# An attention and mixture-of-experts kernel: first expert's preparation in finer steps, its weights split off GpSimd, last pair's rows and the routing's fill in another order

## The chip, the cores and the metric

One core of one Trainium2 chip runs the whole kernel in one launch. The metric is the device time in microseconds (us) of that core; the kernel before takes 794.57 us, the median of three runs (792.56 to 796.7). The engines are named as the profile names them: PE is TensorE (PEld its weight loads), DVE is VectorE, ACT is ScalarE, POOL is GpSimd, SP is SyncE, which here only starts transfers.

## The reference

Three layers are computed one after the other on four sequences (b) of 576 tokens with 512 channels.

```python
# 1. attention, 8 heads of 64: only keys within tau of the row's best score are kept
scores = q @ k.T / 8;  keep = scores >= max(scores) - tau
x = softmax(where(keep, scores, -1e9)) @ v
# 2. mixture of experts: 8 experts, one expert per token
logits = x @ w_gate;   local = sigmoid(x @ w_local)
for s in range(S):                       # a scan along the sequence
    e = argmax(logits[s]) if s == 0 or local[s] < 0.5 else e
    out[s] = softmax(logits[s])[e] * (relu(x[s] @ w1[e]) @ w2[e])
# 3. a second mixture, of 4 causal attention heads, 2 picked per token
```

The choice of the expert is a scan: a token either takes its own best expert or the expert of the token before it.

## The kernel before

**Stage 1, attention (`stage1`).** 32 heads are worked as 16 pairs p. All work of a pair is written as small functions, and each is put at a time on a step axis by `at(g, f, ...)`; the pair p starts at step g = 9p, and the table `W` (line 385) gives the offsets. All functions are then called in the order of their steps, so every engine's queue has that order, and no engine overtakes in its own queue. For a pair, `scores` (PE) gives 9 score tiles, `rowmax` and `keep` (DVE) and `expo` (ACT) make the kept probabilities, `tp` (PE) and `tp_ev` (ACT) transpose them, `av` (PE) multiplies by the values, `rows` (PE, line 334) turns the result into token rows and the routing's logits beside them, `rows_ev` copies these out, and `norm` (line 358) divides by the softmax sums, stores the rows to `x_dram` in HBM and adds the logits into `L`. Pairs 4b to 4b+3 belong to sequence b, so sequences 0 to 2 are complete when pair 11 is through.

**The early routing (`Route.early`, line 509).** While pairs 12 to 15 run, the routing of sequences 0 to 2 is done in 17 pieces which are hooked into stage 1 at the steps of `EARLY` (line 1566): choose the expert per token (`choose`, line 475), transpose, two scans on DVE (`scan`, `ranks`), `count` and `most` (which expert is worked first), `value` and `place` (a token's place among its expert's), `column`, five `hot` (masks, on POOL) and `invert` (15 small PE matmuls that give the list of tokens of the first tile). From `most` comes the first expert's number, with which `weights0` starts its four 1 MB weight transfers (`W0`); `rows0` gathers the first tile's 256 rows (`R0`), `tx0` transposes them (`TX0`), and `split0` (`S0`) splits four 1024-column pieces of the weights into a high and a low part: ACT rounds (line 803), then POOL subtracts (line 804).

**The routing's end (`Route.main`, line 640).** After the last pair, the fourth sequence is routed: a chain of some 60 small DVE instructions with small PE matmuls between them. To keep PE at work, `fill(i)` puts pieces of the first expert's tile (tile 0) into PE's queue at nine places, `FILL[i]` pieces each. The tile has 32 pieces (`start`, line 1025): 16 of the first matrix (six matmuls of 256 columns) and 16 of the second (three of 512). What is not used up in the chain is done after it, with the transposes of tile 1's rows (`tx`) put between at the counts of `LEFT`. `hT_ev` (line 924) takes a finished block of hidden values out of PSUM and splits it; for blocks 0 and 1 (`HPOOL`) POOL does the subtraction. `SPL` tells at which pieces the other four weight pieces (`w2`, line 970 uses them) are split.

**Then** tiles 1 to 8 (`g1`, `g2`) and stage 3 follow; nothing of them is changed.

The order of the last pair before is: its first 256 rows are made at step 149.66 (`rows` p15, after both halves of `av`), its logits in `norm`, as DVE work, and its rows scaled by POOL in one instruction (line 366).

Of the kernel before, what the change touches and what calls it, by code (L numbers as in the profile page):

```python
# [111 lines left out]
def stage1(tc, nc, K, qT, qx, kT, vp, tau, wgl, x_dram, L, X, hooks=(), npair=NP):  # L112
# [14 lines left out]
    iw = C.tile([128, 4, 146], F32, name="iw")  # L127
    nc.gpsimd.memset(iw[:, :, 128:146], 0.0)
    NQ, NK = 3, 2
    QS = [C.tile([128, 2, S], F32R, name=f"QS{i}") for i in range(NQ)]  # L130

    KK = [C.tile([128, 1216], F32R, name=f"KK{i}") for i in range(NK)]
    KL = [C.tile([128, 1216], F32R, name=f"KL{i}") for i in range(NK)]
    KC = (slice(0, 576), slice(576, 1216))
    QM = [C.tile([128, 2, 128], F32R, name=f"QM{i}") for i in range(NK)]

    PD = [C.tile([128, 128], F32, name=f"PD{i}") for i in range(2)]
    J = C.tile([128, 64], F32, name="J")
# [183 lines left out]
    RC, XR, RW, RT = {}, {}, {}, {}  # L322
# [21 lines left out]
    def rows_ev(p, g):  # L344
        t, n = RT.pop((p, g)), 2 + g
        if g == 0:
            XR[p] = (X.tile([128, 5, 2, 64], F32, name="xr", bufs=2),
                     X.tile([128, 5, 2, 9], F32, name="lg", bufs=2))
        tt = t[:, 0:146 * n].rearrange("p (j x)->p j x", x=146)
        js = slice(2 * g, 2 * g + n)  # L350
        if g == 0:
            RW[p] = P1.tile([128, 5, 146], F32, name="xraw", bufs=1)
        nc.scalar.activation(RW[p][:, js], tt, AF.Copy)
        if p == npair - 1:
            nc.vector.tensor_mul(XR[p][1][:, js], tt[:, :, 128:146].rearrange("p j (a d)->p j a d", a=2),
                                 RC[p][:, js].unsqueeze(3).to_broadcast([128, n, 2, 9]))

    def norm(p):
        b, c = divmod(p, 4)
        r, lg = XR[p]  # L360
        q, last = RW.pop(p), p == npair - 1
        if last:
            logits(p, lg, nc.vector)
# [5 lines left out]
        rv = r.rearrange("p j a d->p j (a d)")  # L369
        nc.sync.dma_start(x_dram[b, 0:512, 128 * c:128 * c + 128].rearrange("(j p) d -> p j d", p=128), rv[:, 0:4])  # L370
        nc.sync.dma_start(x_dram[b, 512:576, 128 * c:128 * c + 128], rv[0:64, 4])
        if not last:
            scaled(lg, q[:, :, 128:146], 9)
            logits(p, lg, nc.gpsimd)
# [22 lines left out]
    for p in range(npair):  # L397
# [18 lines left out]
        at(g + W["diag"], diag, p)  # L416
        for h in range(2):
            at(g + W["tpm"][h], tpm, p, h)
            at(g + W["pmev"][h], tpm_ev, p, h)
            for k in range(5):  # L420
                at(g + W["av"][h], av, p, h, k)
            at(g + W["xt"][h], av_ev, p, h)
            at(g + W["row"][h], rows, p, h)
            at(g + W["rev"][h], rows_ev, p, h)
        at(g + W["keep"][8] + 0.1, sums, p)
        at(g + W["recip"], recip, p)
        at(g + W["rev"][1] + 0.1, norm, p)
# [25 lines left out]
class Route:  # L453
# [21 lines left out]
    def choose(self, bs, e=None):  # L475
# [11 lines left out]
        v.scalar_tensor_tensor(fr[:, :, bs], self.L[:, :, bs, 8], Z_THR, s0[:, :, bs], op0=ALU.is_lt, op1=ALU.max)  # L487
        e.tensor_scalar(U[:, 1, :, bs], bc(fr), -1.0, 1.0, op0=ALU.mult, op1=ALU.add)
        v.tensor_reduce(mx[:, :, bs], l8, axis=AX.X, op=ALU.max)
        v.tensor_tensor(q, l8, bc(mx), op=ALU.is_equal)  # L490
        e.tensor_tensor(q, q, w8, op=ALU.mult)
        v.tensor_reduce(m2[:, :, bs], q, axis=AX.X, op=ALU.max)
        v.tensor_tensor(q, q, bc(m2), op=ALU.is_equal)
        e.tensor_tensor(U[:, 0, :, bs], q, bc(fr), op=ALU.mult)
# [14 lines left out]
    def early(self):  # L509
# [9 lines left out]
        def chosen(*_):  # L519
            gp.tensor_copy(self.io, K["iota128"])  # L520
            gp.tensor_copy(K.identb, K["ident"])
            self.choose(slice(0, 3), gp)
# [20 lines left out]
        def scan(*_):  # L543
            O = T["O"] = self.scratch("O")
            v.tensor_tensor_scan(O[rs], T["A"][rs], T["G"][rs], 0.0, op0=ALU.mult, op1=ALU.add)

        def ranks(*_):
            O = T["O"]
            R = T["R"] = self.scratch("R")
            v.tensor_tensor_scan(R[rs], K["ones"][rs, 0:1].to_broadcast([N, S]), O[rs], 0.0, op0=ALU.mult, op1=ALU.add)  # L550

            T["n8"] = E.tile([32, 8], F32, name="n8")
            v.tensor_scalar(T["n8"][rs], K["selE"][rs], R[rs, S - 1:S], None, op0=ALU.mult)
# [69 lines left out]
        def hot(k):  # L623
            def f(*_):
                for b in range(3):
                    gp.tensor_scalar(self.ln[:, k, b], self.io, self.place[:, k, b:b + 1], K["tok"][:, 4 * k + b:4 * k + b + 1],
# [3 lines left out]
        def invert(xt, _):  # L630
            pi = xt()
            for k in range(15):
# [4 lines left out]
        return [chosen, rows("A", 1), rows("G", 0), rest, scan, ranks, count, most, value, place, column,  # L637
                *[hot(k) for k in range(5)], invert]

    def main(self, fill, first):  # L640
# [9 lines left out]
        nc.gpsimd.memset(O[:, S:640], 0.0)  # L650
        fill(0)
        self.choose(slice(3, 4))
# [14 lines left out]
        A = W.tile([32, S], F32, name="A", tag="AR")  # L667
        nc.scalar.activation(A[:, 0:512], pa[0:32], AF.Copy)
        nc.scalar.activation(A[:, 512:S], px[0:32, 128:192], AF.Copy)
        fill(1)  # L670
        v.tensor_copy(selb, K["selb"][0:32])
# [3 lines left out]
        v.tensor_tensor_scan(R, K["ones"][:32, 0:1].to_broadcast([32, S]), O[:, :S], 0.0, op0=ALU.mult, op1=ALU.add)  # L675
        n = R[:, S - 1:S]
# [3 lines left out]
        fill(2)  # L680
# [13 lines left out]
        fill(3)  # L694
# [8 lines left out]
        fill(4)  # L703
# [30 lines left out]
        fill(5)  # L734
# [5 lines left out]
        first()  # L740
        slot = C.tile([128, 20], I32, name="slot")
# [11 lines left out]
        fill(6)  # L753
# [22 lines left out]
        fill(7)  # L776
# [22 lines left out]
def split_chunk(nc, W, src, t, c):  # L799
    tag = "w1" if c < 4 else "w2"  # L800
# [3 lines left out]
    (nc.gpsimd if (t, c) in POOL else nc.vector).tensor_sub(l, src, h.bitcast(F32))  # L804
    return h, l
# [59 lines left out]
def moe(tc, nc, K, R, E, M, yg, W, ctx):  # L865
# [53 lines left out]
    def split(t, c):  # L919
        wc[t, c] = split_chunk(nc, E if c < 4 else W, R.piece(t, c), t, c)  # L920
# [3 lines left out]
    def hT_ev(t, p, i, n, gp=False):  # L924
# [7 lines left out]
        if gp:  # L932
            r = W.tile([128, 512], F32, name="h", bufs=1).rearrange("p (f t) -> p f t", f=2)
            nc.scalar.activation(r, p, AF.Relu)
            nc.gpsimd.tensor_sub(hl, r, hh.bitcast(F32))
        else:
            nc.vector.scalar_tensor_tensor(hl, p, 0.0, hh.bitcast(F32), op0=ALU.max, op1=ALU.subtract)  # L937
# [87 lines left out]
    def start():  # L1025
        hT[0] = []
        for i in range(4):
            p = P1.tile([128, 512], F32, name="acc", bufs=2)
            for k in range(4):
                for f in range(2):  # L1030
                    h_mm(0, p[:, 256 * f:256 * f + 256], 2 * i + f, k, k == 0 and f == 0)
                if k == 3:
                    hT_ev(0, p, i, 0, i in HPOOL)
                for c in range(4, 8):
                    if SPL[c - 4] == 4 * i + k:
                        lab(split, 0, c)
                yield
        ys[0] = [bank("py") for _ in range(2)]
        for i in range(4):
            for u in range(2):  # L1040
                for f in range(2):
                    y_mm(0, i, u, f)
                    if i == 3 and f == 1:
                        y_ev(0, u)
                    yield

    yield
    pieces = start()
# [11 lines left out]
    for i in range(3):  # L1060
        while left > LEFT[i]:
            next(pieces)
            left -= 1
        lab(tx, 1, i)
        gather()
    for _ in pieces:
        pass
# [95 lines left out]
def stage3(tc, nc, K, ws, xr, fetch, xscale, row, out, nb=B):  # L1163
# [380 lines left out]
    for y in range(2 * nb):  # L1544
# [10 lines left out]
        for h, n in enumerate((5, 10)):  # L1555
# [17 lines left out]
SPL = (0, 5, 13, 14)  # L1573
HPOOL = (0, 1)
# [170 lines left out]
```

## Time and profile before

| | us |
|---|---|
| three runs, median (lowest to highest) | 794.57 (792.56 to 796.7) |
| the profiled execution, its own time | 799.57 |
| its span in the trace | 797.8 |
| PE busy | 748.1 (94% of the span) |
| DVE, ACT, POOL busy | 550.2, 490.2, 282.2 |

The profiled execution is 0.6% above the median of the runs; all times of single instructions come from it. A time in the trace counts from the span's start. Stage 1 fills the span up to about 312 us, the routing's end and the rest of tile 0 the stretch to 360.7 us, tiles 1 to 8 and stage 3 what follows. An idle engine costs nothing unless the engine that sets the end waits for it; TensorE's granted clock (1.00 is 2.4 GHz, 0.50 is 1.2 GHz) stands beside the busy times.

### The profile page before, as it was taken

How to read it: one execution, taken by the hardware profiler on the slowest of the kernel's cores; microseconds unless marked ns; L12 is line 12 of the kernel's file. 1: busy time of each engine (PE TensorE's matmuls, PEld its weight loads, DVE VectorE, ACT ScalarE, POOL GpSimd, SP SyncE). 2: the span in 40 equal slices, each digit the busy share in tenths (PEclk: the TensorE clock that was granted, in tenths of full speed). 3: DMA queues.
4: the chain of work that ended last, by engine and by line, in shares of the span. 5: the costliest groups of instructions: out<-in, count | busy, mean ns of one | idle time of the engine just before them, and what ended most of it. 6: DMA issues, size and time to landing. Idle time of an engine off the chain costs nothing. (4 is left out here: it accounts for less than half of the span.)

```text
span 797.8 us, 14293 instructions
## 1 busy us (share of the span) xinstructions
PE 748.1 (94%) x5098; PEld 635.4 (80%) x5098; DVE 550.2 (69%) x1409; ACT 490.2 (61%) x1012; POOL 282.2 (35%) x397
## 2 busy tenths in 40 slices
PE   4999999999997876889999999999978999999997
PEld 3888878888776654779889988998968988898875
DVE  5988888888878844652366446644427889887891
ACT  3788878888775844212455445544425878777784
POOL 5667777677775973250011001100048200000000
PEclk9999999999999978689999999999999999999999
DMA  8339444333431411092455665641024100000102
GB/s 278 130 118 307 121 135 158 121 123 108 138 125 61 183 41 30 1 341 95 169 210 198 212 242 211 206 157 43 18 84 135 39 14 1 28 28 14 54 27 93
DMA packets 37023, 95.69 MB, mean 120 GB/s; under 512 B 4336, under 2 KB 14064, under 8 KB 32848
## 3 DMA queue, kind: packets, MB, share of 16 engines
q1 hardware_dynamic: 31296, 74.77, 27.3%
q0 software_dynamic: 5648, 19.93, 8.0%
q8 instruction: 42, 0.69, 0.4%
q14 instruction: 37, 0.30, 0.1%
HBM read 75.87 MB, written 18.81 MB: 119 GB/s over the span
## 5 line engine op out<-in xcount | busy, mean ns | idle before, releaser
L252 DVE SCALAR_TENSOR_TENSOR P<-S,nm,E 128x576 f32<-128x576 f32 x144 | 116.2, 815 | 10.0 <-ACT E L239 4.0
L229 DVE TENSOR_REDUCE nm<-S 128x1 f32<-128x576 f32 x144 | 106.2, 753 | 19.9 <-PE S L220 19.2
L239 ACT ACTIVATE E<-S,nm 128x576 f32<-128x576 f32 x144 | 104.1, 746 | 10.5 <-DVE nm L229 9.9
L220 PE MATMUL S<-KK,QS 128*128 128x288 f32 x256 | 85.0, 347 | 14.5 <-DVE QS L199 8.9
L265 PE MATMUL X<-cst,P 128*128 128x128 f32 x576 | 88.0, 281 | 0.9 <-ACT PT L276 0.9
L265 PEld LDWEIGHTS X<-cst,P 128*128 128x128 f32 x576 | 67.9, 143 | 16.3 <-issue 7.6
L1601 POOL DMA_INDIRECT xg<-x_dram,inv x22 | 23.0, 1045 | 163.5 <-PE px L909 152.0
L276 ACT ACTIVATE PT<-X 128x512 f32<-128x512 f32 x128 | 75.1, 601 | 8.3 <-PE X L265 4.6
L945 PE MATMUL acc<-xTh,w1l 128*128 128x352 f32 (+1 forms) x256 | 78.0, 305 | 0.0
L945 PE MATMUL acc<-xTh,w1h 128*128 128x352 f32 (+1 forms) x256 | 77.5, 303 | 0.0
L945 PE MATMUL acc<-xTl,w1h 128*128 128x352 f32 (+1 forms) x256 | 77.5, 303 | 0.0
L220 PE MATMUL S<-KL,QS 128*128 128x288 f32 x256 | 73.9, 303 | 0.1
L308 PE MATMUL Y<-PT,v 128*64 128x320 f32 (+1 forms) x512 | 70.7, 419 | 2.4 <-ACT PT L276 1.6
L931 ACT ACTIVATE hTh<-acc 128x352 fp32r<-128x352 f32 (+1 forms) x52 | 26.8, 516 | 73.3 <-PE acc L945 73.3
L970 PE MATMUL py<-w2h,hTh 128*128 128x512 f32 (+1 forms) x176 | 71.7, 407 | 0.0
L937 DVE SCALAR_TENSOR_TENSOR hTl<-acc,hTh 128x352 fp32r<-128x352 f32 (+1 forms) x50 | 29.2, 583 | 60.8 <-ACT hTh L931 60.8
L970 PE MATMUL py<-w2h,hTl 128*128 128x512 f32 (+1 forms) x176 | 69.9, 397 | 0.0
L970 PE MATMUL py<-w2l,hTh 128*128 128x512 f32 (+1 forms) x176 | 69.9, 397 | 0.0
L220 PEld LDWEIGHTS S<-KK,QS 128*128 128x128 f32 x256 | 50.1, 196 | 16.9 <-ACT KK L179 8.9
L308 PEld LDWEIGHTS Y<-PT,v 128*64 128x64 f32 x512 | 34.5, 139 | 28.0 <-issue 6.4
L220 PEld LDWEIGHTS S<-KL,QS 128*128 128x128 f32 x256 | 50.5, 197 | 0.4 <-DVE KL L188 0.4
L1660 POOL DMA_INDIRECT raw<-yg,slot x18 | 17.5, 974 | 92.5 <-DMA yg<-y 62.2
(369 smaller groups left out, 2017.3 us busy)
## 6 DMA issues: line engine op xcount, KB each, us to landing
raw<-in_w_dram SPq DMA_DIRECT2D x32, 1024.0 KB, 5.1
kraw<-in_kT_dram SPq DMA_DIRECT2D x15, 608.0 KB, 4.0
QS<-in_qT_dram POOLq DMA_DIRECT2D x15, 576.0 KB, 4.1
v<-in_vp_dram SPq DMA_DIRECT2D x16, 320.0 KB, 2.9
qraw<-in_qx_dram SPq DMA_DIRECT2D x16, 288.0 KB, 2.9
yg<-y SPq DMA_DIRECT2D x17, 256.0 KB, 4.7
x_dram<-xr SPq DMA_DIRECT2D x16, 256.0 KB, 2.4
yg<-raw SPq DMA_DIRECT2D x1, 3072.0 KB, 13.9
```

What stands on the lines that cost most here:

```text
L220: nc.tensor.matmul(o, QS[p % NQ][:, a, cs], k[i][:, sl(576 * a)], start=(n == 0), stop=(n == 1))
L229: nc.vector.tensor_reduce(nm[:, 0:1], t[:, :, :288], axis=AX.XY, op=ALU.min)
L239: nc.scalar.activation(e, t[:, :, :288], AF.Exp, scale=-1.0, bias=nm[:, 0:1])
L252: nc.vector.scalar_tensor_tensor(PP[p, c][:, S * a:S * a + S].rearrange("p (h n) -> p h n", h=2), t[:, :, :288], nm[:, 1:2], e, op0=ALU.is ...
L265: nc.tensor.transpose(x[:, 128 * kc:128 * kc + 128], pp[:, o:o + 128], ident)
L276: nc.scalar.activation(PT[p, h][:, a, :, f:f + 128], x.rearrange("p (k q) -> p k q", k=4), AF.Copy)
L308: nc.tensor.matmul(out, l, r, start=s, stop=e, skip_group_check=True)
L931: nc.scalar.activation(hh, p, AF.Relu)
L937: nc.vector.scalar_tensor_tensor(hl, p, 0.0, hh.bitcast(F32), op0=ALU.max, op1=ALU.subtract)
L945: nc.tensor.matmul(o, a[:, fs], x[:, k, 0:w], start=(first and n == 0), stop=(k == 3 and n == 2), skip_group_check=True)
L970: nc.tensor.matmul(ys[t][u][0:m], h, w[:, 512 * f:512 * f + 512], start=(i == 0 and f == 0 and n == 0), stop=(i == 3 and f == 1 and n == 2))
L1601: nc.gpsimd.indirect_dma_start(out=o, out_offset=None, in_=src.rearrange("b s d -> (b s) d"), in_offset=bass.IndirectOffsetOnAxis(ap=inv, ...
```

## The change

- **The early routing** becomes 25 pieces: the two constant copies go to step 60, `choose` is cut into six (its DVE and POOL halves apart), each scan into two halves of 288. The steps of `EARLY` are spread: `count` moves from 126.1 to 129.25, `place` from 128.66 to 131.58, `invert` from 137.66 to 142.55. The last `hot` is done by DVE, not POOL. `W0` moves from 126.8 to 129.8, `R0` from 139 to 143, and `TX0` to 146.85 and 147.7.
- **The weight split** of tile 0 happens on DVE except for pieces 0 and 1 (`POOL`). The high part (ACT) and the subtraction have steps of their own. Six pieces, not four, are split in stage 1; 6 and 7 are split in `Route.main` behind the gather of tile 1's rows (`M.splits0`). `SPL` and `HPOOL` are gone: every `hT_ev` is on DVE, and is held back in a list (`M.late`) that `flush` empties at set places of the chain.
- **The last pair**: the first half of its rows is made at step 146.3, before `av`'s second half; its logits are added right after the second half; its rows are scaled by ACT, two and three blocks at a time, ten instructions of 128x64 (`norm_last`).
- **The fill** is (2, 1, 4, 2, 1, 1, 4, 2, 0), 17 pieces, in place of (1, 3, 2, 2, 2, 3, 2, 0), 15. The chain has one more place for it, between the two matmul groups at its start.
- Tiles of stage 1 (`QS`, `KK`, `KL`, `iw`, `PD`, `J`) move into the buffers that the split `w2` pieces use later, so that pieces 4 and 5 can be split in stage 1.

```diff
-    iw = C.tile([128, 4, 146], F32, name="iw")
+    QS = [E2.tile([128, 2, S], F32R, name=f"QS{i}", tag="w2h", bufs=4) for i in range(NQ)]
+    iq = E2.tile([128, 1152], F32, name="iq", tag="w2h", bufs=4)
+    iw = iq[:, 0:584].rearrange("p (c x)->p c x", c=4)
+    KK, KL = ([E2.tile([128, 1216], F32R, name=f"{n}{i}", tag="w2l", bufs=4) for i in range(NK)] for n in ("KK", "KL"))
...
+    def norm_last():
+        q, js = RG.pop(0)
+        for j in range(js.start, js.stop):
+            for a in range(2):
+                nc.scalar.activation(XR[npair - 1][0][:, j, a], q[:, j, 64 * a:64 * a + 64], AF.Copy, scale=RC[npair - 1][:, j, a:a + 1])
+        if not RG and js.start:
+            store(npair - 1)
+    def logits_last():
+        logits(npair - 1, XR[npair - 1][1], nc.vector)
...
+        if p == npair - 1:
+            T = dict(W, row=(11.3, 14.36), rev=(11.7, 14.7), recip=10.6)
+            at(g + 13, norm_last)
+            at(g + 14.71, logits_last)
+            at(g + 14.75, norm_last)
...
-                    gp.tensor_scalar(self.ln[:, k, b], self.io, ...
+                    (v if k == 4 else gp).tensor_scalar(self.ln[:, k, b], self.io, ...
...
         fill(0)
-        self.choose(slice(3, 4))
+        for f in self.choose_steps(slice(3, 4)):
+            f()
         for k, t in ((1, pa), (0, pg)):
...
+            if k:
+                A = W.tile([32, S], F32, name="A", tag="AR")
+                nc.scalar.activation(A[:, 0:512], pa[0:32], AF.Copy)
+                nc.scalar.activation(A[:, 512:S], px[0:32, 128:192], AF.Copy)
+            fill(2 - k)
...
         v.tensor_tensor_scan(R, ...)
+        self.flush()
         small(sm[:, 0:1], K["m1"][0:32], n)
         small(sm[:, 1:2], K["m2"][0:32], n)
-        fill(2)
+        fill(3)
...
         small(tb, K["m3"][0:32], tf)
-        fill(3)
+        fill(4)
+        self.flush()
         v.tensor_tensor(pb, ...)
...
         for j in range(5):
             small(px[:, 276 + 12 * j:288 + 12 * j], O[:, 128 * j:128 * j + 128], ...)
+        fill(6)
...
         v.tensor_tensor(r1, ...)
-        fill(5)
+        self.flush()
...
         v.tensor_scalar(inv[:, 2:], pi, MID, None, op0=ALU.add)
         first()
+        self.M.splits0()
...
-        fill(7)
+        fill(8)
+        self.flush()
...
-    (nc.gpsimd if (t, c) in POOL else nc.vector).tensor_sub(l, src, h.bitcast(F32))
-    return h, l
+    return h, l, lambda: (nc.gpsimd if (t, c) in POOL else nc.vector).tensor_sub(l, src, h.bitcast(F32))
...
-                    hT_ev(0, p, i, 0, i in HPOOL)
+                    M.late.append(lambda p=p, i=i: hT_ev(0, p, i, 0))
+    M.splits0 = lambda: [split(0, c) for c in (6, 7)]
...
-FILL = (1, 3, 2, 2, 2, 3, 2, 0)
-EARLY = (120.5, (122.55, 123), (123.08, 123.4), (124.55, 125), 125.3, 125.8, (126.1, 126.4), 126.7, 126.9, (128.66, 129.2), 129.3,
-         130, 131, 132, 133.25, 134.25, (137.66, 138.3))
-W0 = 126.8
-R0 = 139
-TX0 = ((144.09, 144.4), (146.7, 147.3))
-S0 = (132, 133, 136, 141)
-LEFT = (20, 14, 8)
-POOL = ((0, 0), (0, 1), (0, 2), (0, 3), (0, 4), (0, 5), (0, 6), (0, 7))
+FILL = (2, 1, 4, 2, 1, 1, 4, 2, 0)
+EARLY = (60, 123.4, 123.42, 123.44, 123.46, 124.2, 124.25, (124.55, 125), (125.65, 126.1), (126.12, 126.4), 126.7, 127.2, 127.8, 128.4,
+         (129.25, 129.55), 129.7, 129.9, (131.58, 131.95), 132, 133, 134.5, 136, 137.5, 139, (142.55, 142.9))
+W0 = 129.8
+R0 = 143
+TX0 = ((146.85, 147.25), (147.7, 149.3))
+S0 = ((138.5, 143.2), (140.3, 143.9), (144.7, 145.7), (147.4, 147.9), (147.5, 148.2), (147.6, 148.5))
+LEFT = (12, 10, 9)
+POOL = ((0, 0), (0, 1))
```

## Rows read from the trace of the kernel before

**Rows 1.** The page: each engine's busy time and share of the span.

```profile
PE 748.1 (94%) x5098; PEld 635.4 (80%) x5098; DVE 550.2 (69%) x1409; ACT 490.2 (61%) x1012; POOL 282.2 (35%) x397
```

**Rows 2.** By stretch: us, busy PE, PEld, DVE, ACT, POOL (instructions), PE clock, DMA, GB/s.

```profile
205.94:224.38 18.44, 18.41 (x147) 15.37 (x146) 16.46 (x41) 15.27 (x29) 12.12 (x18) 1.00 0.43 134
224.38:245.94 21.56, 19.74 (x144) 15.59 (x143) 16.44 (x44) 15.62 (x31) 13.60 (x23) 0.92 0.20 57
245.94:270.46 24.52, 19.55 (x143) 14.77 (x141) 22.82 (x63) 15.22 (x28) 18.95 (x31) 1.00 0.52 197
270.46:298.03 27.57, 21.32 (x148) 16.37 (x148) 15.26 (x41) 15.63 (x29) 23.69 (x27) 0.81 0.11 30
298.03:312.45 14.42, 11.46 (x84) 7.51 (x82) 4.52 (x13) 7.48 (x17) 2.86 (x8) 1.00 0.08 22
312.45:343.45 31.00, 24.56 (x158) 22.67 (x158) 20.73 (x66) 7.46 (x11) 12.71 (x10) 0.67 0.13 36
343.45:360.69 17.24, 14.90 (x68) 11.99 (x67) 7.72 (x14) 2.99 (x6) 7.15 (x6) 0.90 1.01 388
```

**Rows 3.** PE's waits from 270.46 to 298.03: us in total, times, longest.

```profile
PE Y L634 <- POOL ln L626: 6.0, 6, 3.1
```

**Rows 4.** POOL's timeline there: start, duration, instruction, count.

```profile
275.45 4.67 POOL L804 TENSOR_TENSOR w1l<-raw,w1h 128x1024 fp32r<-128x1024 f32 x2
280.10 4.66 POOL L626 TENSOR_SCALAR ln<-io,place,cst 128x128 f16<-128x128 f16 x6
```

**Rows 5.** DVE's and PE's timeline, 236 to 251; in brackets idle before, and for whom.

```profile
236.68 0.28 DVE L492 TENSOR_REDUCE m<-eq 128x15 f32<-128x120 f32 x1 [2.67 <-POOL eq L491]
238.06 0.40 PE L220 MATMUL S<-KK,QS 128*128 128x288 f32 x1 [1.82 <-DVE P L252]
...
246.34 1.34 DVE L545 TENSOR_TENSOR_SCAN O<-A,G 24x576 f32<-24x576 f32 x1
...
248.26 1.80 DVE L550 TENSOR_TENSOR_SCAN R<-cst,O 24x576 f32<-24x576 f32 x1
250.21 0.19 PE L558 MATMUL Y<-R,cst 24*32 24x1 f32 x2 [1.99 <-DVE R L550]
```

**Rows 6.** DVE's and POOL's timeline in the routing's end, 313 to 347.

```profile
313.83 0.17 DVE L487 SCALAR_TENSOR_TENSOR fr<-L,cst 128x5 f32<-128x5 f32 x1
314.67 2.34 POOL L804 TENSOR_TENSOR w2l<-raw,w2h 128x1024 fp32r<-128x1024 f32 x1 [0.97 <-ACT w2h L803]
315.05 2.01 DVE L493 TENSOR_TENSOR eq<-eq,m 128x40 f32<-128x40 f32 x1
323.33 1.22 DVE L691 TENSOR_TENSOR tf<-tq,tf 32x1 f32<-32x1 f32 x1
324.94 1.99 DVE L698 CAST V<-O 32x64 fp32r<-32x64 f32 x1
342.68 4.16 DVE L780 CAST erow<-fl 1x24 int32<-1x24 f32 x1
```

**Rows 7.** PE's timeline: tile 0's matmuls at full and at half clock; a wait.

```profile
322.56 0.28 PE L945 MATMUL acc<-xTPh,w1l 128*128 128x256 f32 x1
322.68 0.28 PE L945 MATMUL acc<-xTPh,w1h 128*128 128x256 f32 x1
...
329.18 0.42 PE L945 MATMUL acc<-xTPl,w1h 128*128 128x256 f32 x1
329.39 0.41 PE L945 MATMUL acc<-xTPh,w1l 128*128 128x256 f32 x1
...
348.55 0.66 PE L909 MATMUL py<-cst,xg 128*128 128x128 f32 x4 [2.33 <-DVE ex L790]
```

**Rows 8.** Single lines of the program: count, ns least/median/most, first and last start.

```profile
L804 DVE TENSOR_TENSOR w1l<-raw,w1h x28: 1217/1222/1227, 382.6 to 549.4; 128x1024 fp32r<-128x1024 f32 x28
L803 ACT ACTIVATE w2h<-raw x32: 1046/1052/1062, 313.5 to 571.2; 128x1024 fp32r<-128x1024 f32 x32
L284 ACT ACTIVATE PD<-P x32: 242/252/256, 29.5 to 304.6; 64x64 f32<-64x64 f32 x32
L937 DVE SCALAR_TENSOR_TENSOR hTl<-acc,hTh x50: 515/525/692, 336.8 to 571.3; 128x352 fp32r<-128x352 f32 x32, 128x512 fp32r<-128x512 f32 x18
```

More of the change, by code (lines that the diff above doesn't have):

```diff
@@ L358, in norm @@
     def norm(p):
-        b, c = divmod(p, 4)
         r, lg = XR[p]
-        q, last = RW.pop(p), p == npair - 1
-        if last:
-            logits(p, lg, nc.vector)
+        q = RW.pop(p)
         def scaled(o, src, d):
@@ L368, in norm, with store @@
         scaled(r, q[:, :, 0:128], 64)
-        rv = r.rearrange("p j a d->p j (a d)")
+        store(p)
+        scaled(lg, q[:, :, 128:146], 9)
+        logits(p, lg, nc.gpsimd)
+    def store(p):
+        b, c = divmod(p, 4)
+        rv = XR[p][0].rearrange("p j a d->p j (a d)")
         nc.sync.dma_start(x_dram[b, 0:512, 128 * c:128 * c + 128].rearrange("(j p) d -> p j d", p=128), rv[:, 0:4])
         nc.sync.dma_start(x_dram[b, 512:576, 128 * c:128 * c + 128], rv[0:64, 4])
-        if not last:
-            scaled(lg, q[:, :, 128:146], 9)
-            logits(p, lg, nc.gpsimd)
+    def norm_last():
[7 more added lines that the diff above has]
+        logits(npair - 1, XR[npair - 1][1], nc.vector)
     def logits(p, lg, eng):
@@ L541, in rest, with scan, f, ranks @@
             return out
[L543 to L553, printed above, removed]
+        HS = S // 2
+        def scan(i):
+            def f(*_):
+                O = T.get("O") or T.setdefault("O", self.scratch("O"))
+                c = slice(HS * i, HS * i + HS)
+                v.tensor_tensor_scan(O[rs, c], T["A"][rs, c], T["G"][rs, c], O[rs, HS - 1:HS] if i else 0.0, op0=ALU.mult, op1=ALU.add)
+            return f
+        def ranks(i):
+            def f(*_):
+                O = T["O"]
+                R = T.get("R") or T.setdefault("R", self.scratch("R"))
+                c = slice(HS * i, HS * i + HS)
+                v.tensor_tensor_scan(R[rs, c], K["ones"][rs, 0:1].to_broadcast([N, HS]), O[rs, c], R[rs, HS - 1:HS] if i else 0.0,
+                                     op0=ALU.mult, op1=ALU.add)
+                if i:
+                    T["n8"] = E.tile([32, 8], F32, name="n8")
+                    v.tensor_scalar(T["n8"][rs], K["selE"][rs], R[rs, S - 1:S], None, op0=ALU.mult)
+            return f
         def count(xt, _):
@@ L635, in invert @@
             return lambda: v.tensor_scalar(self.inv[:, 0:2], pi[:, 0:2], MID, None, op0=ALU.add)
-        return [chosen, rows("A", 1), rows("G", 0), rest, scan, ranks, count, most, value, place, column,
-                *[hot(k) for k in range(5)], invert]
+        return [copies, *self.choose_steps(slice(0, 3), gp), rows("A", 1), rows("G", 0), rest, scan(0), scan(1), ranks(0), ranks(1),
+                count, most, value, place, column, *[hot(k) for k in range(5)], invert]
     def main(self, fill, first):
@@ L702, in main @@
             small(ps[:, j], V[:, 128 * j:128 * j + 128], selb[:, 2:4])
-        fill(4)
+        fill(5)
         sel2 = W.tile([32, 3, 4], F32, name="sel2")
@@ L752, in main @@
         small(pe[:, 32:34], K["b0"][0:32], tf)
-        fill(6)
+        fill(7)
         erow = C.tile([1, 2 * NT + 1], I32, name="erow")
@@ L799, in split_chunk, with split_high @@
 def split_chunk(nc, W, src, t, c):
+    h, l, rest = split_high(nc, W, src, t, c)
+    rest()
+    return h, l
+def split_high(nc, W, src, t, c):
     tag = "w1" if c < 4 else "w2"
@@ L931, in hT_ev @@
         nc.scalar.activation(hh, p, AF.Relu)
[L932 to L937, printed above, removed]
+        nc.vector.scalar_tensor_tensor(hl, p, 0.0, hh.bitcast(F32), op0=ALU.max, op1=ALU.subtract)
     def h_mm(t, o, fc, k, first):
@@ L1062, in moe @@
             next(pieces)
+            M.flush()
             left -= 1
@@ L1641, in model, with flush @@
             work = moe(tc, nc, K, R, E, M, yg, W, mx)
+            M.late = []
+            def flush():
+                while M.late:
+                    M.late.pop(0)()
             def fill(i):
```

90 lines of the change are left out of this document (44 added, 46 removed).

## The prediction

> **What bounds the kernel now.** I read four views, in this order. The page first: PE is busy for 94% of the span [rows 1], so a saving must come from the 50 us in which PE idles or from stretches at the lower clock. Then the table by stretch [rows 2], cut at the points where a pair's second row block begins on PE. An undisturbed pair (the row that begins at 205.94) takes 18.44 us with PE busy throughout at clock 1.00: PE bounds it. The next three pairs, beside which the early routing runs, take 21.56, 24.52 and 27.57 us, 73.65 in all; the last pair's rest takes 14.42, the routing's end 31.00 with a mean clock of 0.67, and what is left of tile 0 another 17.24. From 360.69 on nothing is changed, and every later tile begins when its forerunner's PE work ends. So the prediction is one number: by how much earlier does tile 1 begin than at 360.69?
>
> Third, the waits and the timelines of these stretches, for who ends last. In the third pair PE waits 6.0 us for the masks of `invert` [rows 3]; POOL makes the last six only after two weight subtractions of 4.67 us together [rows 4]. In the first, DVE waits 2.67 us for POOL's part of `choose` and PE then 1.82 for DVE; in the second, PE waits 1.99 us for the scan `ranks`, which took 1.80 [rows 5]. In the routing's end DVE itself is the chain, and four of its small instructions take 1.2 to 4.2 us [rows 6]. Fourth, PE's own timeline: tile 0's matmuls follow each other in 0.12 us in one stretch and 0.21 in another [rows 7].
>
> **Early routing, three pairs.** Removed: POOL's 4.67 us ahead of the masks, since `split w0` and `w1` now subtract after `invert`, and `w2`, `w3` on DVE; `invert` itself comes five steps later. The 6.0 us wait goes, and with it the half clock behind it (mean 0.81 in that row). `choose` in six pieces stands behind POOL's `merge`, with other DVE work between the halves, so the 2.67 and 1.82 go too, and the clock of 0.92. How far down can these rows go? The second pair ran at 1.00 and its PE was busy for 19.55 us, the routing's matmuls included; three times that is 58.7, the floor, a gain of 15.0. But in the second pair DVE was busy for 22.82 of 24.52 us: there DVE bounds. The scans, `most`, `value` and `place` stay between the same two cuts (steps 125.08 and 134.08), only finer: the halves leave gaps for `rowmax` and `keep`. The second scan took 1.80 where the first, of the same size, took 1.34 [rows 5]; without that 0.5 DVE needs 22.3, and I take this for this pair. So 19.55 + 22.3 + 19.55 = 61.4, a gain of 12.2. The poor end: this pair stays at 24.5 and each of the others keeps 1.5 us of small waits, 66.6, a gain of 7.1. What is late next: `place` on PE, which waits for POOL's two products; they need `count` alone, two steps earlier, so I see cover for them. The weight transfers start three steps (some 7 us) later, but the first use of a weight also moves from step 132 to 138.5, so this costs nothing; behind their register load on SP's queue stands the load of the last pair's `v`, not used before step 144. The gather moves four steps, its transpose at least one and a half (146.85 against 144.09); if the cover were gone, PE would stand before the last `av`, which I count in the 1.5 us of small waits at the poor end. A `hot` on DVE, three masks, lies in the third pair, where DVE was busy for only 15.26 of 27.57.
>
> **Last pair.** Row block one is made before `av`'s second half, which takes its matmuls and copies off the tail; POOL's scaling becomes ten ACT instructions. ACT gets more ahead of the copy that `rows` needs: three high parts at 1.05 and four scalings at 0.25 (a 64x64 copy is the nearest row) [rows 8], 4.2 us, beside `av`'s 20 matmuls of 320 columns on PE, which at 0.12 per 256 columns [rows 7] take 3.0. So the second row block starts about 1 us later than PE could, and two fewer blocks follow it. I value this at 0, with 1.5 us on either side. The other six scalings lie behind the logits, beside DVE's choice of the expert.
>
> A stretch that the rows leave open is what POOL still does there: its two weight subtractions and pair 14's scaling run beside DVE's subtraction for `w2`. A DVE instruction next to a POOL subtraction took 2.01 us, and ended with it, where its neighbours take 0.2 [rows 6]. I cost it at nothing, since nothing that PE or ACT waits for follows it on DVE until the last row blocks are copied out, and keep 2.4 (one POOL subtraction) for the range. The Trainium skill (SBUF — State Buffer, "Who interferes with whom") says that a DVE instruction with two inputs in SBUF is blocked, whole, by a GpSimd one that reads SBUF and began first; the moved subtraction is of that kind. By it the sum would be about 2.4 us longer, if that cover is gone; the trace agrees in the 2.01 us, and does not show the new pair of instructions.
>
> **The routing's end and tile 0.** Terms, from the chain's begin at 313.83 [rows 6] to tile 1:
> - POOL out of the way: 2.01, 1.22 and 1.99 become about 0.2 each [rows 6]: -4.6.
> - The 4.16 us cast held the exponentials, and PE waited 2.33 us for their bank [rows 6, 7]: -2.3.
> - DVE's new work on the chain: two blocks of `hTl` at 0.69 [rows 8] ahead of `ti` and of `pb`, +1.4; the third lies beside four pieces on PE. The subtractions of pieces 6 and 7 stand ahead of `slot` and `q`, 2 x 1.22 [rows 8]: +2.4, with PE idle, since the next fill is queued behind the matmul that waits for `q`. ACT's high parts lie ahead, where ACT is idle for most of 31 us.
> - 17 pieces in the waits, not 15: two of the second matrix fewer behind, each three matmuls of 512 columns, so 0.24 each by the 0.12 of 256: -1.4.
> - Clock. A piece of six matmuls takes 1.27 us at a spacing of 0.21 and 0.70 at 0.12 [rows 7], 0.57 more. A mean of 0.67 over 31.00 us [rows 2] means two thirds of it at 1.2 GHz, so ten of the 15 pieces: 5.7 us, nearly all on the chain, since a fill that is late holds the next small matmul. The new order puts four pieces where DVE works for about 3 us (the second scan; the masks to `r1`): at full clock they fit, at half they are 2 us too long. And the idle PE ahead of `q` may lose the clock again. Bounds 0 and -5.7; I take -2.9.
>
> Sum -7.4; ends -3 (no clock gained, and one more late fill) and -10.2.
>
> **Sum.** -12.2 + 0 - 7.4 = -19.6 on the profiled execution's 799.57 us: 780.0. That execution is 0.6% above the median of the runs, 794.57; scaled by 794.57/799.57, 775. Ends: 15.0 + 1.5 + 10.2 = 26.7 gives 768; 7.1 - 1.5 + 3 = 8.6 gives 786.
>
> **Rivals.**
> - *The clock stays low and DVE bounds the pairs.* Early pairs give 7.1, the routing's end 4.5 (its terms without the clock): 11.6, so 783. For it: the row at 312.45 shows half clock although PE was busy for 24.56 of 31.00 us, and the new order has an idle of over 2 us ahead of `q`. Against: its early fills are denser.
> - *The stall moves.* POOL still has four masks of three, pair 13's scaling and `column` ahead of `invert`; if they end last again, only half of the 6.0 us goes, and DVE's additions in the end eat what POOL's absence gives: 3 us, 791.6, no change. Against: 4.67 us are out of POOL's queue and five steps lie between.
> - *DVE inherits the bill* (the slow side). DVE takes six subtractions (7.3 us), `hTl` (1.4), a `hot` (0.9): 9.6; ACT 4.2 ahead of the last row block. If none of it is hidden and the early pairs give nothing, 13.8 - 4.6 - 2.3 = +6.9: 806.5, scaled 801. It decides once the early pairs give back under 7 us. For it: DVE's 22.82 of 24.52. Against: POOL's wait is plain in the rows, and four of the subtractions fall where DVE was busy for 4.52 of 14.42 us.
> - *Everything fits*: the clock stays full and the pairs reach their floor, 768.
>
> **Chances.** Forecast (770 to 780) 0.58; low clock and DVE-bound pairs (780 to 788) 0.26; everything fits 0.04; the stall moves 0.07; DVE inherits 0.05. What a measurement can tell from no change is about 0.5%, 4 us: below 790.6 the first three, 0.88; the fourth is the same, 0.07; slower 0.05. The range of 767 to 786 holds the forecast, the fits and most of the second.
>
> **What would show it.** Right: no PE wait of over 1 us for the masks; three pairs of some 61 us; no DVE instruction of 2 us from the chain's begin on; tile 1 about 20 us before 360.69, and the time behind it unchanged. Wrong in size: a clock under 0.7 in the routing's end (second rival), or a second pair of 24 us. Wrong in kind: PE idle at `place`, `invert` or `tx0` for more than 3 us, or an ACT queue that holds the last `rows` by more than 2 us.

## The result, and the profile after

The kernel after takes 783.91 us (median of four runs, 783.31 to 785.71) beside 795.12 for the kernel before (792.56 to 796.7): a ratio of 0.9866, 95% interval 0.9834 to 0.9898. The forecast was 775 us in a range of 767 to 786, and faster with a chance of 0.88. The sign and the range held; the size was 9 us too hopeful, and 783.91 lies in the band that the prediction gave to the low clock (780 to 788), not in that of the forecast (770 to 780).

The page of the kernel after, the answer to [rows 1]: PE is busy 3.7 us less, and the span is 16.3 shorter.

```profile
span 781.5 us, 14284 instructions
PE 744.4 (95%) x5098; PEld 631.2 (81%) x5098; DVE 549.6 (70%) x1422; ACT 491.8 (63%) x1020; POOL 263.9 (34%) x385
```

The stretches of the kernel after, with the columns of [rows 2]. The first three are the pairs of the early routing, the fourth the last pair up to the chain's begin, the fifth and sixth the routing's end and the rest of tile 0.

```profile
224.34:242.66 18.32, 17.46 (x139) 13.97 (x137) 16.28 (x44) 14.47 (x29) 13.25 (x21) 1.00 0.24 67
242.66:268.01 25.35, 22.28 (x148) 15.82 (x149) 23.33 (x67) 14.57 (x29) 18.67 (x31) 0.93 0.32 115
268.01:285.13 17.12, 17.12 (x149) 14.14 (x148) 15.75 (x41) 15.32 (x28) 10.84 (x18) 1.00 0.34 130
285.13:306.02 20.89, 14.66 (x95) 9.63 (x94) 9.53 (x18) 13.48 (x30) 9.29 (x12) 0.92 0.14 40
306.02:331.92 25.90, 21.84 (x159) 19.49 (x157) 18.28 (x71) 5.31 (x9) 4.79 (x5) 0.80 0.18 50
331.92:343.74 11.82, 11.82 (x59) 9.66 (x58) 3.52 (x11) 2.29 (x4) 2.83 (x3) 1.00 0.99 384
```

Cut at the same events (us; "second" is another profiled execution of the kernel before):

| stretch | before | second | after | forecast |
|---|---|---|---|---|
| three pairs with the early routing | 73.65 | 71.81 | 60.79 | 61.4 |
| last pair, to the chain's begin (`fr`) | 15.80 | 15.80 | **20.89** | 15.8 |
| chain and tile 0, to tile 1 | 46.86 | 42.45 | 37.72 | 39.5 |
| behind tile 1's begin | 437.11 | 437.36 | 437.76 | 437.1 |

Two stretches gave what was forecast or more. The last pair, valued at nothing, gave 5.1 back. Its rows on DVE, POOL and PE:

```profile
287.69 2.38 POOL L853 TENSOR_TENSOR w1l<-raw,w1h 128x1024 fp32r<-128x1024 f32 x1
290.02 1.26 POOL L365 TENSOR_TENSOR xr<-xraw,rc 128x640 f32<-128x640 f32 x1
...
292.22 2.34 POOL L853 TENSOR_TENSOR w1l<-raw,w1h 128x1024 fp32r<-128x1024 f32 x1
294.51 0.18 POOL L326 COPY RS<-sM 64x1 f32<-64x1 f32 x1
...
295.02 0.20 POOL L329 TENSOR_SCALAR rc<-RS 128x10 f32<-128x10 f32 x1
...
295.25 0.22 DVE L332 RECIPROCAL rc<-rc 128x10 f32<-128x10 f32 x1 [6.84 <-POOL rc L329]
295.38 1.17 DVE L853 TENSOR_TENSOR w1l<-raw,w1h 128x1024 fp32r<-128x1024 f32 x1
296.48 0.19 DVE L357 TENSOR_TENSOR lg<-Y,rc 128x36 f32<-128x36 f32 x1
296.72 1.09 PE L1661 MATMUL Y<-cst,xg 128*128 128x128 f32 x4 [4.40 <-DVE lg L357]
```

Read it from the bottom. PE waits 4.40 us to transpose tile 0's first rows, because the PSUM buffer still holds the last pair's first row block, until DVE has scaled the logits in it (L357). Ahead of that stands a weight subtraction of DVE's own, 1.17 us, and ahead of the reciprocal DVE has waited 6.84 us for POOL's softmax sums (L326 to L329). POOL had these in its queue behind two weight subtractions of 2.38 and 2.34 us, the very two that the change moved there, with pair 14's rows between them. Behind the wait the granted clock is 0.60 from 296 to 300 us.

In the chain no DVE instruction of 2 us that was held by POOL is left, as forecast. Two other things stand there, ahead of `inv` (the token lists of the later tiles) and of `q` (from which each tile's expert is counted):

```profile
322.66 0.41 PE L988 MATMUL acc<-xTPh,w1h 128*128 128x256 f32 x1
322.87 0.41 PE L988 MATMUL acc<-xTPl,w1h 128*128 128x256 f32 x1
...
324.10 0.19 DVE L779 TENSOR_SCALAR inv<-prest 128x32 int32<-128x32 f32 x1 [3.08 <-PE prest L697]
324.20 2.35 DVE L853 TENSOR_TENSOR w2l<-raw,w2h 128x1024 fp32r<-128x1024 f32 x2
327.36 0.20 PE L697 MATMUL prest<-q,cst 32*1 32x23 f32 x2 [3.30 <-DVE q L790]
```

The four pieces of fill ahead of `inv` run at a spacing of 0.21, half clock, as in [rows 7], and DVE waits 3.08 us for PE; then DVE subtracts two weight pieces (2.35) and PE waits 3.30 for `q`. The second wait belongs to the kernel, the first to this execution: in the repeat below it is 0.70.

### The profile page after: what moved, and what is told of

The parts are those of the page before. It is cut to its first block, busy times and chain, and to the rows that moved or that the text cites. A ratio compares the mean times of both kernels' runs of the same rounds, so it can differ in the third digit from the quotient of the medians.

```text
span 781.5 us, 14284 instructions
## 1 busy us (share of the span) xinstructions
PE 744.4 (95%) x5098; PEld 631.2 (81%) x5098; DVE 549.6 (70%) x1422; ACT 491.8 (63%) x1020; POOL 263.9 (34%) x385
```

## The experiments

All were run with the kernel before beside them. Ratios are against that, with 95% intervals:

| run | us | ratio | interval |
|---|---|---|---|
| after, again | 784.31 | 0.9862 | 0.9838 to 0.9886 |
| sums first | 781.81 | 0.9820 | 0.9799 to 0.9842 |
| sums first, DVE's subtraction of piece 2 later | 783.03 | 0.9848 | 0.9816 to 0.9880 |
| late split | 783.41 | 0.9849 | 0.9824 to 0.9874 |
| late split, late use of the gather | 778.98 | 0.9792 | 0.9764 to 0.9820 |
| fill behind `inv` | 780.54 | 0.9823 | 0.9794 to 0.9853 |
| early routing: products off `most` | 785.32 | 0.9867 | 0.9838 to 0.9897 |
| before, masks ahead of splits | 795.25 | 0.9984 | 0.9966 to 1.0003 |
| last pair mended alone | 779.22 | 0.9805 | 0.9788 to 0.9822 |
| **last pair mended and late split** | **774.04** | **0.9730** | 0.9701 to 0.9759 |
| the same, no split on POOL | 774.18 | 0.9761 | 0.9736 to 0.9785 |

The twelfth run is the second profile of the kernel before. Where a time is compared with "the kernel after", 784.1 is meant, the middle of its two medians (783.91 and 784.31).

The repeat of the kernel after, whose profiled execution takes 783.31 us again, shows the waits of 4.41 and 3.30 us, but not the one ahead of `inv`. DVE there, and the whole chain:

```profile
322.46 0.19 DVE L779 TENSOR_SCALAR inv<-prest 128x32 int32<-128x32 f32 x1 [0.70 <-PE prest L697]
...
307.13:343.68 36.55, 32.49 (x215) 27.69 (x214) 21.82 (x81) 7.60 (x13) 7.64 (x8) 0.91 0.50 178
```

Its last pair takes 21.70 us and its chain 36.55. The half clock has moved: from 316 to 324 us the clock is 1.00 (0.66 and then 0.50 in the first execution), and behind the wait for `q`, from 328 to 332, it is 0.50. An experiment that is read from one execution has to be held against both.

**1. Sums ahead of the subtractions.** POOL's two subtractions get a later step than its sums:

```diff
-S0 = ((138.5, 143.2), (140.3, 143.9), (144.7, 145.7), ...
+S0 = ((138.5, 145.05), (140.3, 145.1), (144.7, 145.7), ...
```

> The changed kernel, with POOL's subtractions of weight pieces 0 and 1 moved from steps 143.2 and 143.9 to 145.05 and 145.1, behind the last pair's sums (144.98); nothing else. Theory (POOL's queue: the sums, and so the reciprocal and the scaled logits that free the PSUM buffer, stand behind two subtractions of 2.36 us): the reciprocal's idle of 6.8 us on DVE falls under 3, PE's wait of 4.40 us falls under 0.7, the av behind it runs at full clock (2.4 instead of 3.6 us), and the time falls by 4.5 to 6 us against the changed kernel, to 0.979 to 0.981 of before. Rival one (ACT's queue, 4.2 us more ahead of the last copy, holds the stretch): PE's wait moves behind the second half of av, and the time falls by under 1.5 us. Rival two (the gathered rows come late): the wait stays at tx0, now released by a transfer, no change.

Half came: 2.5 us below the median of the repeat, PE's wait 2.10 instead of 4.40. The reciprocal is 2.5 us earlier, but the instruction that PE needs stands behind another one. DVE and POOL in that kernel:

```profile
292.79 0.22 DVE L332 RECIPROCAL rc<-rc 128x10 f32<-128x10 f32 x1 [2.37 <-POOL rc L329]
292.92 3.35 DVE L853 TENSOR_TENSOR w1l<-raw,w1h 128x1024 fp32r<-128x1024 f32 x1
296.19 0.18 DVE L357 TENSOR_TENSOR lg<-Y,rc 128x36 f32<-128x36 f32 x1
...
292.83 5.64 POOL L853 TENSOR_TENSOR w1l<-raw,w1h 128x1024 fp32r<-128x1024 f32 x2
```

DVE's subtraction of one piece takes 3.35 us where it takes 1.17 in the kernel after, and POOL's two take 5.64 where one takes 2.34. They run one after the other: 2.34 of POOL and 1.17 of DVE make 3.5, and POOL's second has waited about 1 us.

**2. DVE's subtraction later too** (that of piece 2 at step 147.3, behind the logits of the first row block).

> The kernel after, with the first w1 pieces' split times set so that GpSimd's subtractions for pieces 0 and 1 stand behind the sums of the last pair, and that VectorE's subtraction for piece 2 stands behind the last pair's reciprocals. Theory (the last pair's +5.1 us is sums queued behind subtractions on GpSimd, and, once that is mended, a VectorE subtraction that is held by GpSimd's one, 3.35 instead of 1.17 us): TensorE's wait at the first gather matmul of tile 0 falls from 4.4 us to under 0.7, the stretch behind it stays at full clock, and the time is 5 to 6 us below the kernel after (some 778.5 to 779.5). Rival (the 3.35 us were a delay for another reason, or the subtraction only meets the next GpSimd operation): the wait stays at 2 us or more and the time at 781 to 782, as with the sums alone.

The wait at the transpose is gone and the last pair takes 16.49 us in place of 20.89. But four of DVE's subtractions (5.55 us) and ACT's high parts now stand in front of the last logits, and PE waits there:

```profile
297.76 1.01 PE L340 MATMUL Y<-iq,XT 128*128 128x146 f32 x6 [1.51 <-ACT XT L320]
300.35 0.58 PE L988 MATMUL acc<-xTPh,w1h 128*128 128x256 f32 x1 [1.57 <-DVE lg L357]
```

Behind these two waits the granted clock is 0.50 from 300 to 304, the chain takes 39.57 us (37.72 and 36.55 in the kernel after), and the median is just 1.1 us below the kernel after. The theory named the wait rightly and the gain wrongly: the work had been moved in the queues, not taken out of them.

**3. The remaining split behind the ranks' last small matmul** (`M.splits0()` moved from behind `first()` to ahead of `po`).

> The changed kernel, with the split of weight pieces 6 and 7 (two subtractions of 1.18 us on DVE) moved from ahead of slot and q to behind the small matmul of lt; nothing else. Theory (the two subtractions stand on the chain while PE has nothing queued): PE's wait of 3.3 us for q falls to about 1, and the time falls by 2 to 2.6 us against the changed kernel, 0.983 to 0.984 of before. Rival (the chain's end waits for something else, or the subtractions are only moved to another place of the chain): under 0.7 us.

The wait for `q` falls from 3.30 to 1.03 us, yet tile 1 begins at 343.93, as in the kernel after, for PE now reaches tile 1's gathered rows before they have landed:

```profile
335.73 0.71 PE L957 MATMUL px<-cst,xg 96*128 96x96 f32 x3 [2.87 <-DMA xg<-x_dram,inv]
```

The gathers share the DMA engines with six weight loads. The transfers issued from 318 to 345, with KB each where it is known and the median us to landing:

```profile
raw<-in_w_dram SPq DMA_DIRECT2D x6, 1024.0 KB, 14.9
...
xg<-x_dram,inv POOLq DMA_INDIRECT x7, 8.4
```

**4. The same with tile 1's transposes later** (`LEFT = (10, 7, 4)`).

> The kernel after, with the remaining splits behind the small matmul of the ranks (as in the run with the late split) and tile 1's transposes taken up later in the fill, so that the gathered rows have landed. Theory (the late split does free the chain of 2.3 us, and gave it back as a wait for the gathered rows): the 2.87 us wait for the rows goes, q's wait stays near 1 us, and the time is 2 to 2.6 us below the kernel after (some 781.5). Rival (the work is merely moved: TensorE then lacks fill elsewhere): an idle of 2 us or more turns up somewhere else behind the routing's end and the time is within 1 us of the kernel after.

The wait for the rows is gone and the chain takes 32.83 us, 4.9 less than in the kernel after and 3.7 less than in its repeat; the time is 5.1 us below it, twice what was expected. The other half goes with the clock: its mean over the chain is 0.95 in this run, 0.86 in the kernel after and 0.91 in the repeat.

**5. Two pieces of fill moved from ahead of `inv` into the wait for `q`** (`FILL` 4 to 2 there, two more behind `M.splits0()`).

> The kernel after, with two of the four pieces of fill that stand ahead of the product of the prefix sums moved into TensorE's idle ahead of q. Theory (VectorE's 3.08 us wait for TensorE there is two pieces of fill at half clock that stand on the path): the 3.08 us wait falls to about 0.5, TensorE's 3.30 us wait for q is filled by the two pieces, and the time is 2 to 2.6 us below the kernel after (some 781.5). Rival (the chain is bound by VectorE's subtraction w2l, which keeps its place and its end): q comes no earlier, the idle is filled but something else waits, and the time is within 1 us of the kernel after.

PE's wait for `q` falls from 3.30 to 1.48 and the time by 3.6 us. DVE's wait ahead of `inv` falls from 3.08 to 0.34, but in the repeat of the kernel after it is 0.70 without any edit, so the theory's first half holds for one execution alone. Beside the repeat, PE comes to `q` 18.2 us behind the chain's begin in place of 18.6, and to tile 1 another 15.3 us later in place of 18.0, now at a clock of 1.00. So what is sure of the gain is the filled idle ahead of `q` and the half clock that does not follow it.

**6. The early routing's second pair.** It takes 25.35 us after and 24.52 before; `most`'s small reductions stand beside POOL's products and subtractions. DVE and POOL of the kernel after:

```profile
256.10 1.44 DVE L608 SCALAR_TENSOR_TENSOR te<-te 32x8 f32<-32x8 f32 x1
257.58 1.46 DVE L608 SCALAR_TENSOR_TENSOR te<-te,cst 32x8 f32<-32x8 f32 x1
...
256.13 1.39 POOL L625 TENSOR_TENSOR Ve<-Ve,O 24x576 fp32r<-24x576 f32 x1
257.60 2.93 POOL L197 TENSOR_TENSOR QS<-qraw,QS 64x576 fp32r<-64x576 f32 x2
```

The edit issues POOL's products right behind `count` and DVE's `most` 1.75 steps later, and with it the start of the weight transfers.

> The kernel after, with the early routing's two products on GpSimd issued right behind the count of ranks, and VectorE's reduction and its neighbours (the step `most`) a little later, so that they do not run beside GpSimd's products. Theory (the second pair of the early routing, 25.35 us, still pays for VectorE operations that GpSimd holds: 1.44 and 1.46 us where 0.21 is usual, and for the half clock behind them): both reductions take about 0.2 us, the stretch falls to 22 to 23.5 us, and the time is 2 to 3.5 us below the kernel after (some 781). Rival (the reductions are hidden behind TensorE's scores and the stretch is bound by the two scans and by the pair's own thresholds): the stretch stays within 0.7 us of 25.35 and the time within 1 us.

The stretch falls by 0.8 us and the time does not. POOL's queue is full until 256, so the products start no earlier; DVE's instructions meet POOL's next work instead, the split of a later pair's queries:

```profile
258.36 1.41 DVE L605 SCALAR_TENSOR_TENSOR te<-te,cst 32x8 f32<-32x8 f32 x1
...
258.31 2.94 POOL L197 TENSOR_TENSOR QS<-qraw,QS 64x576 fp32r<-64x576 f32 x2
```

So what the held reductions cost the stretch stays unmeasured.

**7. The kernel before with the masks ahead of three splits** (`S0 = (138.4, 138.5, 138.6, 141)`).

> The kernel before, with one part alone: the first three weight splits move from steps 132, 133 and 136 to 138.4, 138.5 and 138.6, behind the masks and invert; the fourth stays. Theory (POOL's two subtractions ahead of the last six masks were the third pair's stall): PE's wait of 6.0 us for the masks falls under 1.5 us, the third pair of 27.57 us falls to under 22, and the time falls by 5 to 8 us, unless the three subtractions, now bunched, hold POOL's next work, which would give 1 to 3 us back. Rival (the masks are late anyhow, behind POOL's own other work): the wait stays over 4 us, the time within 1.5 us of before.

No change in time, though the third pair takes 24.65 us in its profile where it took 27.57 (26.53 in the second profile of the kernel before). PE's wait for the masks falls from 6.0 us to 2.4, between what the two theories said, and a wait of 1.35 for `inv` appears behind it; the chain takes 47.21 us in this profile, at a mean clock of 0.78. Taking POOL's 4.67 us out of the way is not enough alone, for PE still comes before the masks are through, of which POOL makes the last nine in 7.02 us; which of the other edits (a mask group on DVE, the finer steps, the later `invert`) brings the stretch down to the 17.12 after was not taken apart.

**8. The kernel before, a second profile.**

> The kernel before once more, for a second profiled execution. Theory (the first profiled execution, 799.6 us, lies 4.5 us above the median of its runs by chance of execution): this one's lies nearer to 795, with the same waits and a difference of some us spread over the stretches ahead of tile 1 or in the experts. Rival (the profiler itself adds 4 us to this kernel): it lies again at 799 to 800.

793.35 us, against 799.57 in the first. The waits are the same, one apart (3.55 us for the 2.33 of [rows 7]). The routing's end and tile 0, columns as in [rows 2]:

```profile
311.69:342.68 30.99, 21.35 (x172) 19.22 (x173) 25.44 (x73) 8.46 (x14) 16.77 (x11) 0.94 0.31 95
342.68:354.14 11.46, 11.46 (x47) 9.16 (x46) 2.50 (x6) 1.69 (x3) 1.89 (x2) 0.86 1.02 418
```

42.45 us with a clock of 0.94 and 0.86 (0.92 over the whole), where the first profile had 46.86 with 0.67 for most of it [rows 2] (0.75 over the whole). It is the same kernel with the same instructions; PE is busy for 32.81 us in this stretch where it was for 38.44, and the waits are no shorter, so the 4.4 us are the clock's.

**9. Both mended.** From experiment 4, with the sums first and DVE's subtraction of piece 2 later, as in experiment 2, and with pieces 4 and 5 out of the last pair and into DVE's wait ahead of `inv`:

```diff
-S0 = (..., (144.7, 145.7), (147.4, 147.9), (147.5, 148.2), (147.6, 148.5))
+S0 = ((138.5, 145.05), (140.3, 145.1), (144.7, 147.3), (147.4, 147.9))
...
+    M.splits1 = lambda: [split(0, c) for c in (4, 5)]
...
+        self.M.splits1()
         self.flush()
         pi = px[:, 340:340 + NC]
```

> The kernel after, with the sums of the last pair ahead of GpSimd's subtractions, the splits of pieces 4 and 5 moved from the last pair to VectorE's wait for the prefix product, those of pieces 6 and 7 behind the ranks' small matmul, and tile 1's transposes later. Theory (the sums-first kernel lost half of its gain to ScalarE and VectorE splits bunched ahead of the last logits, 1.51 and 1.57 us of wait and a half clock behind them; the late split's gain, 4.5 us, adds to it): the two waits fall below 1 us together, the stretch from the last pair's second row block to the chain is under 16.5 us, and the time is 773.5 to 775.5 us, below both kernels. Rival (the half clock follows wherever TensorE is first kept waiting, so that gains of the two do not add): 777 to 779, as with the late split alone.

774.04 us, as expected, and 1.3% below the kernel after. The early pairs, the last pair and the chain:

```profile
224.04:284.83 60.79, 56.73 (x432) 43.93 (x431) 55.36 (x151) 44.31 (x85) 42.77 (x69) 0.97 0.30 105
284.83:299.76 14.93, 12.97 (x95) 8.89 (x94) 8.00 (x17) 11.81 (x28) 9.37 (x12) 1.00 0.20 57
299.76:332.50 32.74, 29.51 (x215) 25.34 (x214) 23.70 (x83) 9.49 (x15) 7.63 (x8) 1.00 0.43 151
```

The last pair takes 14.93, 6.0 less than in the kernel after, and the clock is 1.00 from there to tile 1; the one wait over 1 us in this part is 2.47 for `q`.

**10. The last pair alone** (experiment 9 without the late split and the later transposes).

> The kernel of the combined run (774.0 us) with the late split of pieces 6 and 7 and the later transposes of tile 1 taken back, so that only the last pair differs from the kernel after: sums first, pieces 4 and 5 split in VectorE's wait for the prefix product. Theory (the last pair's +5.1 us came from the order of sums and splits alone, and the two gains add): the stretch from the last pair's second row block to the chain stays at 14.5 to 15.5 us against 20.9 of the kernel after, and the time is 5 to 6 us below the kernel after, 778 to 779. Rival (the late split is what keeps the clock up, so that the last pair's gain is lost without it): half clock returns behind the wait for q and the time is 781 to 783.

779.22: the pair alone gives 4.9 us, the late split alone gave 5.1 (experiment 4), both 10.1. They add; in ratios to the kernel before, 0.6%, 0.7% and 1.3%. The last pair takes 14.92 us, as the theory has it. The rival's half clock comes too: both DVE groups of 2.35 us stand ahead of `q` here, PE waits 4.73, and the chain takes 39.93 us at a mean clock of 0.83.

**11. All subtractions on DVE** (`POOL = ()` in the kernel of 9).

> The kernel of the combined run (774.0 us) with the subtractions of pieces 0 and 1 on VectorE too, ahead of the last pair's reciprocals. Theory (a VectorE subtraction of two tiles is held while GpSimd runs one: 3.23 us for two beside GpSimd's, 2.35 alone): the pair for pieces 2 and 3 takes 2.35, the two more fit into VectorE's 2.55 us of idle ahead of the reciprocals or delay these by under 0.5, the chain begins 0.5 to 1 us earlier, and the time is 773 to 773.6. Rival (VectorE's idle is shorter than the two subtractions, since they too are held by GpSimd's normalization): the reciprocals come 1 to 2.5 us later, TensorE waits for its transposes' buffer again, and the time is 775 to 777.

As fast as 9, and in between the theories: the reciprocal comes 1.5 us later in the pair, as the rival says, but the pair takes only 0.3 us longer (15.25). DVE's pair for pieces 2 and 3 takes 2.35 (3.23 in 9), but the other pair delays the sums, since now POOL is the one that is held:

```profile
289.94 3.00 DVE L854 TENSOR_TENSOR w1l<-raw,w1h 128x1024 fp32r<-128x1024 f32 x2
294.11 0.22 DVE L332 RECIPROCAL rc<-rc 128x10 f32<-128x10 f32 x1 [1.17 <-POOL rc L329]
...
289.29 1.27 POOL L365 TENSOR_TENSOR xr<-xraw,rc 128x640 f32<-128x640 f32 x1
290.51 1.34 POOL L365 TENSOR_TENSOR lg<-xraw,rc 128x90 f32<-128x90 f32 x1
291.92 1.14 POOL L394 TENSOR_TENSOR lg<-lg 128x45 f32<-128x45 f32 x1
```

POOL's 90-element product takes 1.34 us here and 0.33 after, its 45-element sum 1.14 and 0.27.

## Why the prediction was right, and where it was off

**Early routing, -12.2: measured -12.9** (-11.0 against the second profile of the kernel before). Right in the sum, not in its parts. No wait for the masks [rows 3] is left, and the first and third pair take 18.32 and 17.12 us, under the floor of 19.55 that was taken for them. The floor was PE's busy time in the second pair; theirs is 17.46 and 17.12. The second pair takes 25.35, not 22.3. The term was DVE's 22.82 us of work less 0.5 for the slow scan, with no idle. But DVE works 23.33 us: the slow scan in two halves takes 1.82 in all, as before, and one more small reduction of `most` is held beside POOL's work, 1.46 us where it took 0.21. For the other 2.0 us DVE is idle.

```profile
249.57 0.91 DVE L583 TENSOR_TENSOR_SCAN R<-cst,O 24x288 f32<-24x288 f32 x1
...
252.11 0.91 DVE L583 TENSOR_TENSOR_SCAN R<-cst,R,O 24x288 f32<-24x288 f32 x1
```

That the early pairs gave the time is read from their rows; which of the edits gave how much of it no run shows, and the one that was tried alone (experiment 7) changed nothing in the time.

**Last pair, 0 ± 1.5: measured +5.1.** This is the step that failed. It looked at ACT and at DVE's subtraction and said that "nothing that PE or ACT waits for follows it on DVE until the last row blocks are copied out". That is not so: the scaling of the first block's logits (L357) follows it, and the first row block, made earlier, holds a PSUM buffer that PE needs next until this is done. Of the 4.40 us about 1.1 are DVE's own subtraction. The larger part is what the prediction did not ask: what follows the two moved subtractions on **POOL**, namely the sums of the last pair, by which the logits are scaled. Its own sign of being wrong in kind, PE idle at `tx0` for more than 3 us, came. Experiments 1, 2 and 9 take the 5.1 us back in three steps (19.5, 16.5 and 14.9 us for this stretch) by the order and place of these instructions alone; at 14.9 the stretch is 0.9 shorter than before the change, inside the 1.5 that was given.

**Routing's end, -7.4: measured -9.1** on the profiles, -4.7 against the second profile of the kernel before. POOL's terms and the 2.33 us wait went as forecast. The +2.4 for the two subtractions ahead of `q` stands in the trace as 2.35, and experiments 3 and 4 show that it was on the path. Of the clock, the four pieces of fill of which it says that "at half they are 2 us too long" came, as a 3.08 us wait for PE, but in one execution of two (0.70 in the repeat). What set the clock's fall near 317 us, with PE busy for 3.97 of 4 us, no run shows. It is not the 4.40 us wait 20 us earlier, for the repeat has that wait, 4.41 us, and holds 1.00 there.

**From the profile to the runs.** The sum on the profiled execution was 780.0, its own time 783.31: off by 3.3, which is the last pair's 5.1 and the 0.65 behind tile 1's begin, less the 0.7 and 1.7 that the other stretches gave beyond the forecast. The scaling to 775 added 5 more. It took the first execution's excess of 5 us over the median as spread evenly; the second profile, 6.2 us shorter, differs just in the stretches that the change replaces, 4.4 in the chain and 1.8 in the early pairs. The kernel after has no such excess (783.31 is the lowest of its runs), so the gain in the runs is 11.2 and not 16.3.

**The rivals.** Of "the clock stays low and DVE bounds the pairs" (783) the second pair and the half clock came, though the early pairs gave their full 12.9 and not its 7.1, and the routing's end 9.1 and not its 4.5. Its time is right by luck: these two stretches gave 10.4 us more than it said, and the 5.1 us lost in the last pair and the 5 us of the scaling, neither of them among its reasons, made up for that. The masks did not stall again, and DVE did not become the bound of the whole.

**The rule that was weighed.** The hold between DVE and POOL did not occur at the place that the prediction bounded: DVE's subtraction took 1.17 us there, POOL being done. It occurs in the second pair and in experiments 1, 2, 9 and 11. The Trainium skill (SBUF — State Buffer, "Who interferes with whom") has it that issue order decides which of the two is blocked, and that the block is whole. The trace agrees both ways: 3.35 us for DVE's 1.17 (experiment 1), 1.34 for POOL's 0.33 (experiment 11).

## What to carry to other kernels

When an instruction is moved behind another on the same engine, list what stands behind its new place and which buffer that releases: here three small sums behind two moved subtractions cost 5.1 us. A stretch valued at nothing deserves the same list as one valued at ten, and a mended wait should be followed to the next instruction of the same queue before its gain is counted. Take the base of a forecast from two executions where the granted clock differs, and see in which stretch they differ before scaling. The same holds for an experiment that is to remove a wait: see first whether the wait stands in a second execution.

## What was not expected of the hardware

- The mean granted clock of one and the same stretch, the chain and tile 0, was 0.75 in one execution and 0.92 in another (kernel before), and the time of the stretch differed by 4.4 us. After PE had waited 4.73 us (experiment 10) the clock read 0.50 from 320 to 328 us although PE was busy for 7.9 of these 8 us:

```profile
316.00:320.00 4.00, 0.00 (x0) 0.00 (x0) 3.93 (x10) 0.00 (x0) 2.40 (x2) 0.71 0.07 16
320.00:324.00 4.00, 3.90 (x19) 3.08 (x19) 2.72 (x17) 0.60 (x1) 2.25 (x3) 0.50 0.67 173
324.00:328.00 4.00, 4.00 (x14) 3.45 (x14) 2.01 (x9) 0.34 (x1) 0.00 (x0) 0.50 0.97 331
```

- A DVE instruction on 32x8 elements took 1.44 us beside a POOL product of 1.39, its neighbours 0.15: the hold goes by the other engine's instruction, not by the size of one's own.
- Gathered rows took 8.4 us to land (median) beside six weight loads of 1 MB, 5.5 over the whole run, so the place of their first use has to follow the traffic.
